# Thirty rows of wo a partition instead of thirty-one, and GpSimd loads part of the remainder

## The chip, the core and the metric

The kernel runs on one core of a Trainium2 chip. The core has five engines that are ordered among themselves only by semaphores: TensorE (PE, with weight loads shown as PEld), VectorE (DVE), ScalarE (ACT), GpSimd (POOL) and SyncE (SP, which only issues loads and stores here), and sixteen DMA engines that move data between the memory (HBM) and the core's own memory of 128 partitions. The metric is device time in microseconds: the median of several runs without a profiler. The profile is of one execution more.

## What is computed

One step of attention for 32 sequences (`B`), 32 query heads that share 8 key and value heads, head width 128, over the last 512 of 2048 cached positions, with a projection before (`wq`) and behind (`wo`):

```python
W = min(4096, max(256, Sk // 4))                      # 512
q = (x @ wq).reshape(B, Sq, Hq, Dh)                   # heads ahead of positions
k = jnp.repeat(k_cache[:, :, Sk - W:, :], rep, axis=1)
v = jnp.repeat(v_cache[:, :, Sk - W:, :], rep, axis=1)
p = softmax(einsum("bhqd,bhkd->bhqk", q, k) * Dh ** -0.5)
o = einsum("bhqk,bhkd->bhqd", p, v)
return o.reshape(B, Sq, Hq * Dh) @ wo                 # wo: 4096 rows of 512
```

All data are bf16. Nearly all bytes are the two caches (32 MB each); `wq` and `wo` have 4 MB each.

## The kernel before

The 32 sequences are worked in eight groups `q` of four (`NQ`). For each group there is a load `K{q}` of 4 MB into one of two buffers `K_sb`, and a load `V{q}` into one of two buffers `V_sb`; V5 to V7 are cut in two pieces. SyncE issues all of them in the order of the list `LOADS`, on one queue: a load is issued when its buffer is free (K waits for the transposes `T` of the group two before, V for the products `P` of the group two before), and the DMA engines work on loads in the order in which they were issued. SyncE's own order is therefore the order of all big loads: a wait in it holds back every load behind it.

VectorE transposes K (`KT_sb`, line 538), TensorE makes the scores (`S`, line 362), VectorE and ScalarE the softmax, TensorE turns the weights into value rows (`E`, line 376) and multiplies with V (`P`, line 388); VectorE and ScalarE copy the sums (`C_sb`), and a fold (`F`, lines 398 and 404) on TensorE and a copy `D` on ScalarE (line 598) bring the attention's output of the group into `o_sel`, laid out for the last projection. The order on each engine is written out in the lists at the top.

**The last projection.** Row `128 h + r` of `wo` belongs to head `h` and place `r` of its output. Partition `4 h + d` of `wo_sb` holds `NI` = 31 rows of head `h`, rows `31 d` to `31 d + 30`: 128 partitions, 124 rows of each head. `wo_sb` lies in the first K buffer, which is free once T6 is done; it is loaded in three pieces W0, W1, W2 of 21, 8 and 2 rows a partition (`WOP`), the last loads of the kernel. The `NX` = 4 rows of each head that are left over go to a tile `wx_sb` of their own, all four of a head in one partition, 4 KB. They are brought by seven small loads A0 to A6 (`EXTRA`: first head, last head, first partition), each of five heads (the last of two), to partitions that lie four apart. These stand in `LOADS` behind V5.1. `wx_sb` has rows in 32 partitions only; the rest is zero, by a memset on GpSimd early in the program (line 305), and the small loads wait for it (`pool_w`).

`fold` follows the same split: four matrices times 31 columns (`F_sb`, line 398) for the rows in `wo_sb`, and one matrix `F_x` (line 404) that puts each head's four remaining columns where `wx_sb` has its rows. GpSimd builds `F_x` with three copies (line 315). `o_sel` has `NI + NX` columns for each sequence.

At the end TensorE waits for the last copy D and for all small loads (`sem_wx`), multiplies with the `NX` rows of `wx_sb` (four products a row, line 485), then waits for W0, W1 and W2 in turn and multiplies with their rows. For W2 the products are ordered so that half of the output is finished first; VectorE and ScalarE copy a half each, and SyncE and ScalarE store them.

**GpSimd** builds masks and constants, and for each pair of groups copies the queries from `QT_sb` into `QBD` (line 328, sixteen copies; the last four wait for the scores of group 5). After those it has nothing to do. `QT_sb` holds 4096 elements a partition and is read by nothing else.

```python
EXTRA = [(5 * j, min(5 * j + 5, 32), j + 28 * (j // 4)) for j in range(7)]
WOP = [(0, 21), (21, 29), (29, 31)]
```

Of the kernel before, what the change touches and what calls it, by code (L numbers as in the profile page):

```python
# [5 lines left out]
BF16 = mybir.dt.bfloat16  # L6
# [22 lines left out]
ROUNDS = 3  # L29

LOADS = """
K0 K1 V0.0 K2 V1.0 K3 V2.0 K4 V3.0 K5 K6 V4.0 K7 V5.0 V5.1 A0 A1 A2 A3 A4 A5 A6 V6.0 V6.1 V7.0 V7.1 W0 W1 W2
""".split()

X_PARTS = [(0, 25), (25, 30), (30, 32)]
V_PIECES = 5 * [[0, 32]] + 2 * [[0, 16, 32]] + [[0, 18, 32]]
EXTRA = [(5 * j, min(5 * j + 5, 32), j + 28 * (j // 4)) for j in range(7)]
WOP = [(0, 21), (21, 29), (29, 31)]


def ops_of(text):
# [3 lines left out]
def bass_standalone__sliding_block_cached__sampling_kernel(  # L45
# [7 lines left out]
):  # L53
    B, Sq, D = x.shape
    _, HKV, SK, DH = k_cache.shape
    HD = wq.shape[1]
    HQ = HD // DH
# [3 lines left out]
    P = 128  # L61
# [2 lines left out]
    NQ = B // 4  # L64
    KB = 4
    R = W // KB
    NI = 31
    NX = DH - 4 * NI
    LAST = NQ - 1
    PIECES = 4  # L70
# [56 lines left out]
    with ExitStack() as es:  # L127
        sb = lambda name, shape, dt: es.enter_context(nc.sbuf_tensor(name, shape, dt))
        sem = lambda name: es.enter_context(nc.semaphore(name))
# [8 lines left out]
        QT_sb = sb("QT_sb", [P, 32, 2, HQ, 2], BF16)  # L138
# [3 lines left out]
        PTc = sb("PTc", [P, R, REP], BF16)  # L142
        C_sb = sb("C_sb", [P, 2, 4, DH], F32)
        o_sel = sb("o_sel", [P, NI + NX, 8 + B], BF16)
        wx_sb = sb("wx_sb", [P, NX, D], BF16)
        E_sb = sb("E_sb", [P, REP, 33, KB], BF16)
        F_pad = sb("F_pad", [P, 4 * (4 * HQ + 1)], F32)
        F_x = sb("F_x", [P, P], F32)
# [7 lines left out]
        wq_sb = V_sb[1][:, :].rearrange("p (kt n) -> p kt n", kt=DKT)  # L156
        wo_sb = K_sb[0][:, 0:NI * D].rearrange("p (i n) -> p i n", i=NI)

# [7 lines left out]
        F_hd = spare[:, 1792:1856].bitcast(F32)  # L166
# [9 lines left out]
        def folds(q):  # L176
            return (F_ps if q < LAST - 1 else O_ps[:, q - LAST + 1])[:, 0:4 * (NI + NX)].rearrange(
                "p (b i) -> p b i", b=4)
# [6 lines left out]
        sem_k = [sem(f"sem_k{i}") for i in range(2)]  # L185
        sem_v = [[sem(f"sem_v{i}_{j}") for j in range(max(len(v) for v in V_PIECES) - 1)] for i in range(2)]
        sem_wx = sem("sem_wx")
        sem_wo = [sem(f"sem_wo{i}") for i in range(len(WOP))]
        sem_out = sem("sem_out")
        names = (  # L190
# [3 lines left out]
        s = {n: sem(n) for n in names}  # L194
# [44 lines left out]
        @block.sync  # L239
        def _(sp):  # L240
            wait = Waits(sp)
            wo_h = wo.rearrange("(h r) n -> h (r n)", r=DH)
            wo_r = wo_h[:, 0:4 * NI * D].rearrange("h (d m) -> h d m", d=4)
            wx = wx_sb.rearrange("p a n -> p (a n)")
            for op in ops_of(" ".join(LOADS)):
                kind, q = op[0], op[1]
                if kind == "K":
                    if q == 2:
                        for key, n in BIAS.items():
                            sp.sem_inc(op_sem[key], n)  # L250
                    if q >= 2:
                        wait([ends["T", q - 2, 1]])
                    sp.dma_start(K_sb[q % 2][:, :], rows(k_cache, q)).then_inc(sem_k[q % 2], 16)
                elif kind == "V":
                    if q == 1:
                        sp.wait_ge(s["pe_q"], 8)
                    r0, r1 = (4 * g for g in V_PIECES[q][op[2]:op[2] + 2])
                    if q >= 2:
                        wait([ends["P", q - 2, r1 // 4 - 1]])
                    sp.dma_start(  # L260
                        V_sb[q % 2][:, r0 * DH:r1 * DH], rows(v_cache, q, r0, r1)
                    ).then_inc(sem_v[q % 2][op[2]], 16)
                    if q and len(V_PIECES[q]) == 2:
                        sp.sem_inc(sem_v[q % 2][1], 16)
                elif kind == "A":
                    h0, h1, p0 = EXTRA[q]
                    sp.wait_ge(s["pool_w"], 1)
                    sp.dma_start(
                        wx[p0:p0 + 4 * (h1 - h0) - 3:4, :], wo_h[h0:h1, 4 * NI * D:]
                    ).then_inc(sem_wx, 16)  # L270
                else:
                    wait([ends["T", NQ - 2, 1]])
                    i0, i1 = WOP[q]
                    sp.dma_start(
                        wo_sb[:, i0:i1, :].rearrange("p i n -> p (i n)"),
                        wo_r[:, :, i0 * D:i1 * D],
                    ).then_inc(sem_wo[q], 16)
            store(sp, 0)

        @block.gpsimd  # L280
        def _(pool):
            wait = Waits(pool)

            def diag(t, pattern, name):
                pool.memset(t, 0.0).then_inc(s[name], 1)
                pool.wait_ge(s[name], 1)
                pool.affine_select(
                    out=t, in_=t, compare_op=ALU.not_equal, fill=1.0,
                    base=0, pattern=pattern, channel_multiplier=1,
                ).then_inc(s[name], 1)  # L290

            diag(xsel[:, :, :], [[-1, 4], [-4, 32]], "pool_x")
            pool.memset(junk[:, :], 0.0).then_inc(s["pool_j"], 1)
            pool.memset(QBD[:, :, :, :], 0.0).then_inc(s["pool_q"], 1)
            diag(F_id[:, :, :], [[-1, HQ], [-32, 4]], "pool_f")
            diag(m_id[:, :, :, :], [[-4, HKV], [-32, 4], [-1, KB]], "pool_m")
            pool.memset(F_pad[:, :], 0.0).then_inc(s["pool_fz"], 1)

            diag(E_id[:, :, :].rearrange("p e (b h) -> p e b h", b=4),
                 [[-1, REP], [-4, 4], [-16, HKV]], "pool_ei")  # L300
            pool.memset(E_sb[:, :, :, :], 0.0).then_inc(s["pool_e"], 1)
            pool.wait_ge(s["pool_e"], 1)
            pool.wait_ge(s["pool_ei"], 2)
            pool.tensor_copy(E_sb[:, :, 0:32, KB - 1], E_id[:, :, :]).then_inc(s["pool_e"], 1)
            pool.memset(wx_sb[:, :, :], 0.0).then_inc(s["pool_w"], 1)
            pool.memset(F_x[:, :], 0.0).then_inc(s["pool_fz"], 1)
            pool.wait_ge(s["pool_e"], 2)
            pool.wait_ge(s["pool_fz"], 2)
            pool.wait_ge(s["dve_c"], 1)
            pool.tensor_copy(  # L310
                F_diag, F_hd.unsqueeze(1).to_broadcast([P, 4, HQ])
            ).then_inc(s["pool_fz"], 1)
            for h0, h1, p0 in ((0, 20, 0), (20, 30, 32), (30, 32, 34)):
                k = min(5, h1 - h0)
                pool.tensor_copy(
                    F_x[:, p0:p0 + 20].rearrange("p (k l) -> p l k", l=4)[:, 0:(h1 - h0) // k, 0:k],
                    F_hd[:, h0:h1].rearrange("p (l k) -> p l k", k=k),
                ).then_inc(s["pool_fz"], 1)
            pool.wait_ge(s["pool_q"], 1)
            pool.wait_ge(s["dve_QT"], 1)  # L320
            for q in range(0, NQ, 2):
                if q:
                    wait([ends["S", q - 1, 1]])
                for b in range(4):
                    pr = slice(32 * b, 32 * b + 32)
                    if q or b:
                        pool.wait_ge(s["pool_qbd"], 2 * q + b)
                    pool.tensor_copy(  # L328
                        QBD[pr].rearrange("p u a (h c) -> p u a h c", h=HKV).rearrange(
                            "p u (w t) h c -> p (u w) t h c", w=2)[:, :, :, :, 4 * b:4 * b + 4],  # L330
                        QT_sb[pr, q:q + 2].rearrange("p u w (h e) t -> p (u w) t h e", h=HKV),
                    ).then_inc(s["pool_qbd"], 1)

        @block.tensor
        def _(pe):
# [124 lines left out]
            with pe.Fori(0, ROUNDS) as j:  # L460
                for op, site in zip(rounds[0], steps):
                    waits = []
                    for key in sorted({key for w, _ in site for key in w}):
# [9 lines left out]
                        a, b = fits[-1]  # L473
# [4 lines left out]
            wait = Waits(pe)  # L478
            wait([ends["D", NQ - 1]])
            pe.wait_ge(sem_wx, 16 * len(EXTRA))  # L480

            def summed(i, rows, cs):
                for c in cs:
                    n = 2 * (c % 2) + c // 2
                    ins = pe.matmul(  # L485
                        Y_ps[32 * c:32 * (c + 1), 0:P],
                        lhsT=o_sel[:, i, 8:], rhs=rows[:, n * P:(n + 1) * P],
                        start=i == NI, stop=i == NI - 1, tile_position=(0, 32 * c),
                    )
                return ins  # L490

            for i in range(NX):
                summed(NI + i, wx_sb[:, i], range(4))
            for j, (i0, i1) in enumerate(WOP):
                pe.wait_ge(sem_wo[j], 16)
                last = j == len(WOP) - 1
                for cs in ((0, 1), (2, 3)) if last else (range(4),):
# [169 lines left out]
```

## Time and profile before

| | |
|---|---|
| time, median of 3 runs | 183.33 us (183.27 to 183.37) |
| time of the profiled execution | 183.41 us |
| its span, first to last instruction | 182.1 us |
| TensorE busy | 123.3 us (68%) |
| VectorE busy | 108.9 us (60%) |
| ScalarE, GpSimd busy | 46.8 us, 14.7 us |
| moved | 75.68 MB, 416 GB/s over the span |
| chain that ended last, by engine | DMA 52%, DVE 19%, PE 18%, issue 7% |

Times are from the first instruction on, the span lies inside the measured time, and the profiled execution was 0.08 us longer than the median. Where the profile shows the span in forty slices, each digit is the busy share of one slice (4.55 us) in tenths. A line of the chain of waits has start, duration and what was being worked on or waited for, in us. A line of the timeline has start, duration, engine, line of the kernel, operation, tile written and tiles read, count, and in brackets the idle time before it and what ended that.

### The profile page before, as it was taken

The numbers are of one execution on the slowest core, as the hardware profiler recorded it, in microseconds if no ns is written. First come the engines' busy times: TensorE is split into PE (matmuls) and PEld (weight loads), VectorE is DVE, ScalarE is ACT, GpSimd is POOL, SyncE is SP. The second block draws the span as 40 slices with busy tenths as digits, with TensorE's granted clock in tenths as the row PEclk, the third lists the DMA queues.
The fourth block names the chain that finished last, engine by engine and source line by source line (L and its number), as shares of the span: only waits on it lengthen the run. The fifth ranks groups of instructions, "written<-read, shape, count | busy, mean of one in ns | idle before, by whom it ended". The sixth has DMA issues, their size and how long they took to land.

```text
span 182.1 us, 3916 instructions
## 1 busy us (share of the span) xinstructions
PE 123.3 (68%) x1664; PEld 60.5 (33%) x1664; DVE 108.9 (60%) x103; ACT 46.8 (26%) x85; POOL 14.7 (8%) x39
## 2 busy tenths in 40 slices
PE   0029900444499879728992799645199899699984
PEld 0013300113135255205440355204035454354463
DVE  0022289849959950997079814997942499824030
ACT  3000310016014422601062014402006416327030
POOL 7910003000030000003000000002000000000000
PEclk9999995555559969965799559965559999999999
DMA  6998999999999999999999999999999999999992
GB/s 236 462 425 389 453 461 432 389 446 461 435 389 439 457 425 400 439 461 414 403 446 450 417 410 446 453 418 410 446 446 389 428 428 436 422 435 429 446 377 77
DMA packets 3523, 75.68 MB, mean 416 GB/s; under 512 B 444, under 2 KB 540, under 8 KB 700
## 3 DMA queue, kind: packets, MB, share of 16 engines
q1 hardware_dynamic: 3424, 75.52, 97.0%
q8 instruction: 7, 0.11, 0.3%
q10 hardware_dynamic: 92, 0.05, 0.1%
HBM read 75.53 MB, written 0.03 MB: 415 GB/s over the span
## 4 chain that ended last, share of the span: by engine, by line
DMA 52%; DVE 19%; PE 18%; issue 7%; ACT 1%; DVEq 1%; SPq 0%; ACTq 0%
DMA K_sb<-in_k_cache_dram 16%; DMA V_sb<-in_v_cache_dram 16%; DVE KT_sb L538 16%; DMA K_sb<-in_wo_dram 13%; PE ps L388 8%; DMA V_sb<-in_wq_dram 7%; PE ps L350 5%; PE ps L362 3%; DVE QT_sb L526 2%; PE ps L376 1%; PE ps L398 1%; ACT KT_sb L588 1%; PE ps L485 1%; DVEq L571 0%; DVE maxv L552 0%
## 5 line engine op out<-in xcount | busy, mean ns | idle before, releaser
L538 DVE STREAM_TRANSPOSE KT_sb<-K_sb 128x4096 f32<-128x4096 f32 x16 | 70.2, 4424 | 17.0 <-DMA K_sb<-in_k_cache_dram 16.9
L388 PE MATMUL ps<-V_sb,bd 32*128 32x512 bf16 x1024 | 66.5, 415 | 6.6 <-DMA V_sb<-in_v_cache_dram 6.6
L362 PE MATMUL ps<-KT_sb,QBD 128*32 128x512 bf16 x256 | 22.5, 487 | 29.4 <-DVE KT_sb L538 29.4
L388 PEld LDWEIGHTS ps<-V_sb,bd 32*128 32x128 bf16 x1024 | 27.0, 101 | 40.8 <-issue 10.5
L619 ACT ACTIVATE bd<-PTc,mask 128x512 bf16 x32 | 20.5, 710 | 1.5 <-ACT PTc L614 1.5
L362 PEld LDWEIGHTS ps<-KT_sb,QBD 128*32 128x32 bf16 x256 | 6.2, 108 | 43.2 <-DVE KT_sb L538 34.5
L605 ACT ACTIVATE P_f<-ps,negmax 128x512 f32<-128x512 f32 x8 | 5.5, 687 | 51.7 <-DVE negmax L554 51.7
L398 PE MATMUL ps<-C_sb,F_pad 128*128 128x124 f32 x64 | 12.6, 358 | 4.9 <-DVE C_sb L550 4.6
L614 ACT ACTIVATE PTc<-ps 128x512 bf16<-128x512 f32 x8 | 4.8, 597 | 39.7 <-PE ps L376 39.7
L328 POOL COPY QBD<-QT_sb 32x256 bf16<-32x256 bf16 x16 | 6.2, 390 | 105.1 <-PE ps L362 90.1
L398 PEld LDWEIGHTS ps<-C_sb,F_pad 128*128 128x128 f32 x64 | 10.7, 253 | 9.5 <-DVE C_sb L550 8.7
L571 DVE TENSOR_SCALAR bd<-PTc,mask 128x512 bf16 x32 | 8.9, 342 | 7.6 <-ACT PTc L614 7.6
L376 PE MATMUL ps<-P_bf,E_sb 128*128 128x128 bf16 x128 | 9.5, 234 | 2.6 <-DVE P_bf L561 2.6
L350 PE MATMUL ps<-V_sb,bd 128*128 128x512 bf16 x32 | 9.1, 456 | 2.0 <-DMA V_sb<-in_wq_dram 2.0
L376 PEld LDWEIGHTS ps<-P_bf,E_sb 128*128 128x128 bf16 x128 | 8.1, 105 | 6.9 <-DVE P_bf L561 3.5
L626 ACT ACTIVATE C_sb<-ps 32x512 f32<-32x512 f32 x14 | 8.2, 588 | 8.2 <-PE ps L388 8.1
L550 DVE COPY C_sb<-ps 32x512 f32<-32x512 f32 x12 | 8.3, 693 | 2.9 <-PE ps L388 2.6
L339 PE MATMUL ps<-bd 32*128 32x128 bf16 x4 | 0.6, 294 | 10.6 <-DMA bd<-in_x_dram 10.6
L552 DVE TENSOR_REDUCE maxv<-ps 128x1 f32<-128x512 f32 x8 | 5.5, 691 | 3.6 <-PE ps L362 3.4
L578 DVE COPY C_sb<-ps 32x512 f32<-32x512 f32 x4 | 2.8, 693 | 8.1 <-PE ps L388 8.0
L510 DVE CAST bd<-ps 128x512 bf16<-128x512 f32 x1 | 0.7, 691 | 11.2 <-PE ps L339 11.2
L521 DVE CAST KT_sb<-ps 128x1024 bf16<-128x1024 f32 x2 | 2.4, 1224 | 7.1 <-PE ps L350 7.1
(37 smaller groups left out, 44.1 us busy)
## 6 DMA issues: line engine op xcount, KB each, us to landing
K_sb<-in_k_cache_dram SPq DMA_DIRECT2D x8, 4096.0 KB, 22.5
V_sb<-in_v_cache_dram SPq DMA_DIRECT2D x5, 4096.0 KB, 26.4
V_sb<-in_v_cache_dram SPq DMA_DIRECT2D x4, 2048.0 KB, 21.5
V_sb<-in_wq_dram SPq DMA_DIRECT2D x1, 4096.0 KB, 12.3
K_sb<-in_wo_dram SPq DMA_DIRECT2D x1, 2688.0 KB, 21.7
V_sb<-in_v_cache_dram SPq DMA_DIRECT2D x1, 2304.0 KB, 14.2
V_sb<-in_v_cache_dram SPq DMA_DIRECT2D x1, 1792.0 KB, 15.8
K_sb<-in_wo_dram SPq DMA_DIRECT2D x1, 1024.0 KB, 23.5
```

The costliest lines, as they stand in the source:

```text
L328: pool.tensor_copy(QBD[pr].rearrange("p u a (h c) -> p u a h c", h=HKV).rearrange("p u (w t) h c -> p (u w) t h c", w=2)[:, :, :, :, 4 * b ...
L350: ins = pe.matmul(ps[:, n], lhsT=xT_sb[:, kt, :], rhs=wq_sb[:, kt, n * 512:(n + 1) * 512], start=kt == 0, stop=kt == DKT - 1, tile_positio ...
L362: ins = pe.matmul(S_ps[32 * c:32 * c + 32, :], lhsT=QBD[:, q % 2, 2 * w + t, c0:c0 + 32], rhs=KT_sb[:, w, :, KB * h:KB * h + KB, t], start ...
L376: ins = pe.matmul(EP_ps[:, e * R:(e + 1) * R], lhsT=window[:, KB - 1 - k:KB - 1 - k + P], rhs=P_bf[:, k * R:(k + 1) * R], start=k == 0, st ...
L388: ins = pe.matmul(sums_of(b, q), lhsT=bd[pr, q % 2, 4 * g:4 * g + 4].rearrange("p r h e -> p (r h e)"), rhs=V_sb[q % 2][pr, 512 * g:512 * ...
L398: ins = pe.matmul(folds(q)[:, :, 0:NI], lhsT=F_sb[:, d].rearrange("p h d -> p (h d)"), rhs=C_sb[:, q // LAST, :, NI * d:NI * d + NI], star ...
L538: dve.transpose(KT_sb[:, w].bitcast(F32).rearrange("p r c t -> p r (c t)"), K_sb[i].bitcast(F32).rearrange("p (r w c) -> p r w c", r=R, w= ...
L550: dve.tensor_copy(*pick_args(r)).then_inc(op_sem["ANY", "C"], 1)
L552: dve.tensor_reduce(maxv[:, :], S_ps, AX.X, ALU.max).then_inc(s["dve_m"], 1)
L571: ins = dve.tensor_scalar(bd[:, bass.ds(odd, 1), :, h, :].rearrange("p o r e -> p (o r) e"), PTc[:, :, :], mask[:, h:h + 1], None, op0=ALU ...
L619: ins = act.activation(bd[:, bass.ds(odd, 1), :, h, :].rearrange("p o r e -> p (o r) e"), PTc[:, :, :], ACTF.Copy, scale=mask[:, h:h + 1])
L626: act.activation(*pick_args(r), ACTF.Copy).then_inc(op_sem["ANY", "C"], 1)
```

## The change

`NI` becomes 30, so `wo_sb` has 120 rows of each head, W0 has 20 rows a partition instead of 21, and `NX` is 8. A head's eight remaining rows are 8 KB in one partition.

`wx_sb` is no tile of its own any more but the memory of `QT_sb`. Its memset, twice as wide, moves from GpSimd's start to behind the last copy into `QBD`, for which it waits (`pool_qbd` 16).

The small loads on SyncE become five, A0 to A4: five heads each for heads 0 to 19, and four for heads 24 to 27. The rows of the other eight heads, 20 to 23 and 28 to 31, are brought by one load that GpSimd issues, to partitions 60 to 67. Its source has the form 2 x 4 x 8 KB. Ahead of it and behind it GpSimd issues a load of seven rows of 64 bytes into a scratch tile `passed`, which nothing reads; GpSimd waits for both at its end. TensorE waits for GpSimd's load too (`sem_w2`) before it multiplies with `wx_sb`. `F_x` follows the new partitions with three copies as before.

```diff
-K0 K1 V0.0 K2 V1.0 K3 V2.0 K4 V3.0 K5 K6 V4.0 K7 V5.0 V5.1 A0 A1 A2 A3 A4 A5 A6 V6.0 V6.1 V7.0 V7.1 W0 W1 W2
+K0 K1 V0.0 K2 V1.0 K3 V2.0 K4 V3.0 K5 K6 V4.0 K7 V5.0 V5.1 A0 A1 A2 A3 A4 V6.0 V6.1 V7.0 V7.1 W0 W1 W2
...
-EXTRA = [(5 * j, min(5 * j + 5, 32), j + 28 * (j // 4)) for j in range(7)]
-WOP = [(0, 21), (21, 29), (29, 31)]
+EXTRA = [(5 * j, 5 * j + 5, j) for j in range(4)] + [(24, 28, 32)]
+PASSED = (7, 7)
+WOP = [(0, 20), (20, 28), (28, 30)]
...
-    NI = 31
+    NI = 30
...
-        wx_sb = sb("wx_sb", [P, NX, D], BF16)
+        wx_sb = QT_sb[:, :, :, :, :].rearrange("p j w h t -> p (j w h t)").rearrange("p (a n) -> p a n", n=D)
+        passed = sb("passed", [16, 32], BF16)
...
-            pool.memset(wx_sb[:, :, :], 0.0).then_inc(s["pool_w"], 1)
...
-            for h0, h1, p0 in ((0, 20, 0), (20, 30, 32), (30, 32, 34)):
-                k = min(5, h1 - h0)
-                pool.tensor_copy(
-                    F_x[:, p0:p0 + 20].rearrange("p (k l) -> p l k", l=4)[:, 0:(h1 - h0) // k, 0:k],
-                    F_hd[:, h0:h1].rearrange("p (l k) -> p l k", k=k),
-                ).then_inc(s["pool_fz"], 1)
+            for to, of in (
+                (F_x[:, 0:20].rearrange("p (k l) -> p l k", l=4),
+                 F_hd[:, 0:20].rearrange("p (l k) -> p l k", k=5)),
+                (F_x[:, 32:48].rearrange("p (k l) -> p k l", l=4)[:, :, 0], F_hd[:, 24:28]),
+                (F_x[:, 60:68].rearrange("p (a g) -> p a g", a=2),
+                 F_hd[:, 16:32].rearrange("p (a g) -> p a g", a=2)[:, :, 4:8]),
+            ):
+                pool.tensor_copy(to, of).then_inc(s["pool_fz"], 1)
...
+            pool.wait_ge(s["pool_qbd"], 16)
+            pool.memset(wx_sb[:, :, :], 0.0).then_inc(s["pool_w"], 1)
+            for n, (a, k) in enumerate(zip((0, 8), PASSED)):
+                pool.dma_start(
+                    passed[a:a + k, :], wo[a:a + k, 0:32]
+                ).then_inc(sem_pass[n], 16)
+                if n == 0:
+                    pool.wait_ge(s["pool_w"], 1)
+                    pool.dma_start(
+                        wx_sb.rearrange("p a n -> p (a n)")[60:68, :],
+                        wo.rearrange("(a g r) n -> a g (r n)", a=4, g=8)[2:4, 4:8, 4 * NI * D:],
+                    ).then_inc(sem_w2, 16)
+            for each in sem_pass:
+                pool.wait_ge(each, 16)
...
             pe.wait_ge(sem_wx, 16 * len(EXTRA))
+            pe.wait_ge(sem_w2, 16)
```

More of the change, by code (lines that the diff above doesn't have):

```diff
@@ L187, in bass_standalone__sliding_block_cached__sampling_kernel @@
         sem_wx = sem("sem_wx")
+        sem_pass = [sem(f"sem_pass{i}") for i in range(len(PASSED))]
+        sem_w2 = sem("sem_w2")
         sem_wo = [sem(f"sem_wo{i}") for i in range(len(WOP))]
```

## The prediction

> **What bounds the kernel now.** I read the page's rows of the sixteen DMA engines first, then the chain of waits in order of time, then the last microseconds of TensorE and the queue of SyncE.
>
> ```profile
> DMA  6998999999999999999999999999999999999992
> q1 hardware_dynamic: 3424, 75.52, 97.0%
> q8 instruction: 7, 0.11, 0.3%
> ```
>
> The DMA engines are busy to nine tenths or more from the third slice to the last but one, and the queue of SyncE and its loads (q1) is 97.0% of sixteen engines' span. So the kernel ends when its last load has landed and a short tail has run. The chain of waits shows the tail:
>
> ```profile
> 155.27 0.32 SPq L274
> 155.59 0.04 issue
> 155.63 23.50 DMA K_sb<-in_wo_dram
> 179.13 0.04 issue
> 179.17 0.97 PE ps L485 x40
> 180.14 0.02 issue
> 180.16 0.27 ACT P_bf L634
> ```
>
> W1, the second of the three loads of wo, lands at 179.13 us. TensorE does 32 products with it and 8 with W2, and the output is copied and stored. The same end on TensorE (start, duration, operation, idle time before):
>
> ```profile
> 177.30 0.41 PE L485 MATMUL ps<-wx_sb,o_sel 128*32 128x128 bf16 x16 [0.38 <-ACT o_sel L598]
> 177.53 1.35 PE L485 MATMUL ps<-K_sb,o_sel 128*32 128x128 bf16 x84
> 179.17 0.90 PE L485 MATMUL ps<-K_sb,o_sel 128*32 128x128 bf16 x40 [0.29 <-DMA K_sb<-in_wo_dram]
> ```
>
> The single records inside these rows: four products start every 56 ns. The last of W0's 84 starts at 178.66, so TensorE could go on at 178.70 and stands still until 179.17. W1's 32 products start from 179.17 to 179.58. The last 8 start at 179.77, because W2 lands at 179.73. W2's last part sets the end.
>
> A load lands in sixteen parts, one for each DMA engine, and the trace keeps the arrival of each. K0's sixteen parts arrive within 0.47 us (22.25 to 22.72). W2's lie 2.06 us apart, in three groups: five **free** parts (177.67 to 178.15), five **row** parts (178.72, 178.75, 178.81, 178.95, 179.23) and six **fetch** parts (179.37, 179.39, 179.40, 179.42, 179.55, 179.73). Two things made the groups. Each of the instruction packets (16 KB, q8) holds up the engine that carries it: it takes 1.06 us, and the 32 KB packet after it takes 1.71 instead of 1.21. After the one at 48.8 us fifteen parts of K2 arrive from 51.39 to 51.86 and one at 53.21; by V5.1, after five such packets, eleven parts arrive from 148.59 to 149.05 and five from 150.29 to 150.68. A sixth comes at 174.2. The other thing is the seven loads of a few rows, queued just behind V5.1: in V6.0, the load after them, five of the eleven early parts are 0.95 to 1.11 us later than their fellows, which is six or seven packets of 4 KB at the 159 ns that each takes. So a load of five rows uses five engines, the same five each time, and none of them is one that fetched.
>
> **The change, part by part.**
>
> *W0 is a row shorter in every partition.* Each engine serves eight partitions, so each loses 8 KB. Packets of 21,504 and 8,192 bytes take 801 and 309 ns: 0.037 ns a byte, 38 ns for 1 KB, 0.30 us for eight packets. W1 and W2 keep their sizes, so every part of both arrives 0.30 earlier. The latest, a fetch part, has nothing added: 179.73 becomes 179.43.
>
> *The row loads.* Five loads of 8 KB rows replace seven of 4 KB rows. The two engines that carried seven packets (1.11 us) carry five of 309 ns (1.55): +0.43, less 0.30, is +0.13. Two that carried six (0.95) get +0.59 less 0.30, +0.29; the last carries four (1.24), +0.28 less 0.30, -0.02. The latest row part (179.23; its slip of 1.11 in V6.0 marks it as one of the seven-packet engines) becomes 179.36. The others end at 179.10 or earlier. So the row parts catch up with the fetch parts but don't pass them.
>
> *GpSimd's load.* Eight rows of 8 KB in two shares put four packets, 4 x 309 = 1.24 us, on two engines. On free ones their parts arrive at 178.15 - 0.30 + 1.24 = 179.09 at the latest: hidden behind 179.43. On engines that are late already they set the end (first rival). The trace has no load issued by GpSimd, so which engines take the shares is its largest unknown. What it shows: six fetches fell on six different engines, none a row engine. That looks like a rotation, which would leave the free five side by side, and neighbours share a fate; and rows ahead that move the start on may move it past the row engines. I take free engines, a little over even.
>
> By the Trainium skill's "DMA: Bandwidth & Descriptors", section "Why a DMA increments its semaphore by 16 and not by 1", a load from SyncE takes the lowest-numbered engines, as many as divide both sides' slowest dimension, and one from GpSimd takes consecutive engines from a cursor that moves round. The five slipped parts of V6.0 agree with the first half; no run here shows the second. By it the seven tiny rows lead the shares to the eighth and ninth engines, if the cursor began at the first, and the sum is what it is above if those two are free.
>
> *The two loads of seven tiny rows.* They put one packet of 64 bytes and some completion writes on an engine. Below: nearly nothing (a 4-byte write takes 9 ns, a 512-byte packet 28). Above: what an instruction packet costs beyond its bytes. It made its engine's part 1.53 late where 16 KB of a load take 0.61, so 0.92. The 1 KB packets of x, sent from another queue between wq's packets, left gaps of 34 to 90 ns. In kind and size these are nearest; I take 0.03, and keep 0.92 as a rival.
>
> *GpSimd and SyncE.* The memset of wx (1.91 us at 6.95) leaves the start, where GpSimd then waits for VectorE until 12.25 anyway: nothing. It returns twice as wide behind the last copies of QBD:
>
> ```profile
> 122.55 1.74 POOL L328 COPY QBD<-QT_sb 32x256 bf16<-32x256 bf16 x4 [37.33 <-PE ps L362]
> ```
>
> and here is what SyncE does at that time:
>
> ```profile
> 122.42 5.10 SPq L268 DMA_DIRECT2D wx_sb<-in_wo_dram  x7
> 138.72 16.22 SPq L260 DMA_DIRECT2D V_sb<-in_v_cache_dram  x4
> ```
>
> The memset runs from 124.3 to about 128.0 (twice 1.8 to 1.9). The row loads, which wait for it, are issued from 128.0 to 131.6 (five at 5.10/7 = 0.73). Queued behind them is V6.0, which waits for TensorE until 138.72: 7 us of cover. Were that gone, V6.0's first packets would still have until about 148.6, when the engines are through with V5.1. GpSimd's own three issues, at 0.5 to 0.9 us each by SyncE's rows or several times that, end forty microseconds before 177.3, when TensorE wants the rows; nothing on its queue waits behind them but the end. VectorE transposes while GpSimd writes: its sixteen transposes took 4.40 to 4.45 us each, GpSimd's copies beside one or not, so nothing.
>
> *TensorE.* 16 products more with wx and 4 fewer with W0: three groups of 56 ns, 0.17. The folds have four columns fewer in eight instructions and 16 more in two: nothing. The copy of o_sel has 152 columns for 140: 0.03 at most. TensorE is ready for W1 at 178.70 + 0.20 = 178.90 instead of waiting; W1's latest part comes at 179.13 - 0.30 = 178.83. Its products end by 179.35, before W2's 179.43. The cover here is 0.1 us: with a gain much above 0.3, TensorE would set the end.
>
> **The sum.** -0.30 + 0.03 = -0.27 on the profiled execution: 183.41 becomes 183.14, its span 182.1 becomes 181.8. The median shown is 183.33, 0.08 under that execution, so the forecast is 183.06 (-0.15%). Its own range, with 0.1 to 0.2 for a lag of the engines that differs between runs, is 182.85 to 183.25. A difference under 0.2%, 0.37 us, is about what a measurement of this kernel can't tell from none.
>
> **The rivals.**
>
> *The shares fall on late engines.* On a fetch engine a share makes W2's part 179.37 to 179.73, less 0.30, plus 1.24: 180.31 to 180.67. On a row engine it is 180.60 for the latest and about 180.3 for the others. It decides from any engine whose part is now later than 179.73 + 0.30 - 1.24 = 178.79, or that gets longer rows besides: eleven of the sixteen. The end comes 0.55 to 0.95 later; V7.1's latest part moves from 170.25 to 171.5 at most, and TensorE, 1.24 later, still reaches W1 at 180.1, before W2. With the later of two shares counting, I take +0.8: 184.1. For it: only five of sixteen engines are free, and nothing in the trace names them. Against: the rotation.
>
> *GpSimd's loads cost every engine what a fetch costs beyond its bytes.* 179.43 + 0.92 = 180.35, +0.62: 183.95. For it: the instruction packets. Against: the packets of x, and that all three are over forty microseconds before the end, though a lag stays once it is there, as K2's late part shows.
>
> *The change doesn't do what it says: the eight rows go one to an engine, from the first.* The latest row part becomes 179.36 + 0.31 = 179.67, with the tiny packets 179.70 against 179.73: 183.30. The same page and section tells of such a spread: some loads from GpSimd take all sixteen engines, with an even number of partitions on each. No run here shows it.
>
> **How the numbers follow.** Forecast 0.52, of which 0.20 ends more than 0.37 us under 183.33 (lags that shrink more than the sum has them) and 0.32 within; late engines 0.30; a cost on every engine 0.12; spread rows 0.06. So faster 0.20, same 0.38, slower 0.42. The time is the forecast's; the range reaches from its lower bound to the first rival's upper one, 182.85 to 184.3.
>
> **What would show it.** Right: W2's parts in two groups instead of three, the latest near 179.45, and two parts near 179.0 that were early; TensorE's wait before W1 gone or under 0.1; V6.0 issued near 138.7 as before. The first rival: one or two parts of every load after about 130 us 1.2 later than the others of their group, and past 180 at the end. The second: all sixteen later together. The third: eight parts with 0.3 more, none with 1.24. I am wrong in the bound itself if W2 lands 0.3 earlier and the end doesn't move, or if SyncE issues V6.0 late.

## The result: 1% slower, and the profile after

| | before | after |
|---|---|---|
| median | 183.35 us (183.27 to 183.51, 4 runs) | 185.25 us (185.08 to 185.36, 4 runs) |
| ratio to before | | 1.0102 (95% interval 1.0084 to 1.0119) |
| profiled execution, its span | 183.41, 182.1 us | 185.08, 183.6 us |
| W2's latest part | 179.73 us | 181.19 us |

The page of the changed kernel has nearly the same row of DMA engines, a little less in q1, and one queue more:

```profile
DMA  6999999989999999999999999999999999999981
GB/s 234 458 450 400 407 457 457 443 378 436 453 450 428 382 450 453 428 407 418 457 439 414 407 450 450 428 421 414 457 364 364 432 425 428 437 428 423 440 365 55
q1 hardware_dynamic: 3408, 75.45, 96.7%
q8 instruction: 7, 0.11, 0.2%
q0 software_dynamic: 144, 0.07, 0.1%
```

In the row of GB/s, two slices in a row show 364; each is 4.6 us, so they are the time from 133 to 142 us. Before the change no slice between the second and the tail was under 389. The DMA engines are as busy as ever in these slices and move less. The chain of waits ends as before, 1.4 to 1.5 us later:

```profile
157.82 22.73 DMA K_sb<-in_wo_dram
180.56 0.04 issue
180.60 0.63 PE ps L505 x32
181.23 0.00 issue
181.24 0.37 PE ps L505 x8
```

TensorE's end (start, duration, idle time ahead in brackets): the wait for W1 did not go, it grew from 0.29 to 0.40 us.

```profile
178.46 0.63 PE L505 MATMUL ps<-QT_sb,o_sel 128*32 128x128 bf16 x32 [0.39 <-ACT o_sel L618]
178.91 1.29 PE L505 MATMUL ps<-K_sb,o_sel 128*32 128x128 bf16 x80
180.60 0.94 PE L505 MATMUL ps<-K_sb,o_sel 128*32 128x128 bf16 x40 [0.40 <-DMA K_sb<-in_wo_dram]
```

Around the moved memset, on GpSimd, SyncE and VectorE:

```profile
124.23 3.51 POOL L339 MEMSET QT_sb<- 128x4096 bf16 x1
...
128.35 0.59 POOL L346 DMA_DIRECT2D QT_sb<-in_wo_dram  x1
...
127.77 3.67 SPq L272 DMA_DIRECT2D QT_sb<-in_wo_dram  x5
138.48 18.65 SPq L264 DMA_DIRECT2D V_sb<-in_v_cache_dram  x4
...
124.90 3.13 DVE L581 TENSOR_SCALAR P_bf<-P_f,recip 128x512 bf16<-128x512 f32 x1
```

SyncE issues V6.0 when it did before. VectorE's product with `recip` takes 3.13 us beside the memset; the seven others of its kind take 0.49.

**Where the 1.46 us on W2 come from.** The arrivals of the parts split it. (The trace doesn't name the engine of a packet. On a busy engine a packet starts within some 10 ns of the end of the one before, and by that the records of one engine can be joined.) Fourteen of W2's parts come by 180.32, two at 181.18 and 181.19. Two things are added up here.

First, every engine lost time while GpSimd's rows were under way. The eight packets of 8 KB run in four rounds, one on each of two engines, at 134.8, 136.5, 138.2 and 140.0 us. In the same time K7's 32 KB packets, on all sixteen engines, take some 1.46 us instead of 1.21, until 141 us; beside the first round it is 1.39. The stretch comes some tenths of a microsecond behind the record of a round: the packet from 135.66 to 136.88 has the second round's record (136.47 to 136.79) inside it and still takes 1.22, and the next on its engine takes 1.47. So each round holds up all engines for 0.17 to 0.25 us. Two engines that carry no share lose 0.1 us more (packets of 1.54 to 1.57); that they are the ones that fill partitions 60 to 67 would fit, but is not shown. K7's earliest parts come at 139.49 instead of 138.81, V5.1's at 149.53 instead of 148.59, and the fourteen parts of W2 at 180.32 where 179.43 was forecast: +0.89.

Second, the two engines that carry the shares are not free ones. Their records hold the four packets of GpSimd and, at 150 us, the five packets of SyncE's row loads. The two loads of seven tiny rows both ran on the same seven engines, and these two are among them. The share and the longer rows together make their parts 0.87 later than the rest. -0.30 + 0.89 + 0.87 = +1.46.

### The profile page after: what moved, and what is told of

It is laid out like the page before. It is cut to its first block, busy times and chain, and to the rows that moved or that the text cites. A ratio compares the mean times of both kernels' runs of the same rounds, so it can differ in the third digit from the quotient of the medians.

```text
span 183.6 us, 3943 instructions
## 1 busy us (share of the span) xinstructions
PE 124.1 (68%) x1676; PEld 61.2 (33%) x1676; DVE 111.5 (61%) x103; ACT 46.8 (26%) x85; POOL 18.1 (10%) x42
## 4 chain that ended last, share of the span: by engine, by line
DMA 62%; DVE 14%; PE 12%; issue 8%; DVEq 1%; SPq 1%; ACT 1%; ACTq 0%
DMA K_sb<-in_k_cache_dram 29%; DMA V_sb<-in_v_cache_dram 14%; DMA K_sb<-in_wo_dram 12%; DVE KT_sb L558 11%; DMA V_sb<-in_wq_dram 7%; PE ps L369 5%; PE ps L407 5%; DVE QT_sb L546 2%; PE ps L381 1%; ACT KT_sb L608 1%; PE ps L395 1%; PE ps L505 1%; DVE maxv L572 0%; SPq L278 0%; SPq L257 0%
## 5 line engine op out<-in xcount | busy, mean ns | idle before, releaser
L407 PE MATMUL ps<-V_sb,bd 32*128 32x512 bf16 x1024 | 67.7, 419 | 7.7 <-DMA V_sb<-in_v_cache_dram 7.5
L381 PE MATMUL ps<-KT_sb,QBD 128*32 128x512 bf16 x256 | 22.0, 479 | 29.9 <-DVE KT_sb L558 29.9
L407 PEld LDWEIGHTS ps<-V_sb,bd 32*128 32x128 bf16 x1024 | 27.5, 102 | 42.7 <-issue 12.2
L417 PE MATMUL ps<-C_sb,F_pad 128*128 128x120 f32 x64 | 12.8, 362 | 3.8 <-DVE C_sb L570 3.5
L581 DVE TENSOR_SCALAR P_bf<-P_f,recip 128x512 bf16<-128x512 f32 x8 | 6.5, 816 | 0.9
```

The lines of the kernel that those rows point to most:

```text
L381: ins = pe.matmul(S_ps[32 * c:32 * c + 32, :], lhsT=QBD[:, q % 2, 2 * w + t, c0:c0 + 32], rhs=KT_sb[:, w, :, KB * h:KB * h + KB, t], start ...
L407: ins = pe.matmul(sums_of(b, q), lhsT=bd[pr, q % 2, 4 * g:4 * g + 4].rearrange("p r h e -> p (r h e)"), rhs=V_sb[q % 2][pr, 512 * g:512 * ...
L417: ins = pe.matmul(folds(q)[:, :, 0:NI], lhsT=F_sb[:, d].rearrange("p h d -> p (h d)"), rhs=C_sb[:, q // LAST, :, NI * d:NI * d + NI], star ...
L581: dve.tensor_scalar(P_bf[:, :], P_f32[:, :], recip[:, :], None, op0=ALU.mult).then_inc(done("N"), 1)
```

## The experiments

Ratios are to the kernel before on the same chip, with their 95% intervals.

### The rows without GpSimd, and GpSimd's tiny loads without the rows

`e1_sp_rows`:

```diff
-K7 V5.0 V5.1 A0 A1 A2 A3 A4 V6.0
+K7 V5.0 V5.1 A0 A1 A2 A3 A4 A5 A6 V6.0
...
+[(20, 24, 32), (24, 28, 33), (28, 32, 34)]      # EXTRA behind the first four
-            for n, (a, k) in enumerate(zip((0, 8), PASSED)):
...
-            pe.wait_ge(sem_w2, 16)
```

> The changed kernel without any load from GpSimd: the eight heads' rows come by two more small loads from SyncE (four heads each, seven small loads in all, partitions 32 to 47). The changed kernel's trace shows all sixteen parts of K7 0.7 to 1.0 us later than before, while GpSimd's rows are under way. Theory 'GpSimd's load stalls every engine': without it K7's parts are back at 138.8 to 139.05 and 140.5 to 140.9, W0 is 0.30 us shorter for every part, and the end is set by the four engines that carry seven rows of 8 KB (7 x 0.309 = 2.16 us instead of 1.11): 179.23 + 1.05 - 0.30 = 179.98 us for W2, time 183.6. Rival 'the memset, or the late transposes behind it, do it' (VectorE's product with recip took 3.13 us beside the memset instead of 0.49): K7's parts stay late, time 184.5.

183.76 us, ratio 1.0018 (1.0008 to 1.0028). K7's parts are back at 138.93 to 139.25 and 140.51 to 140.81, with the memset and its 3.12 us product still there. W2's latest four parts come at 179.90 to 180.02, where 179.98 was worked out. So the memset isn't the cause, and the prices of the shorter W0 and of an 8 KB row hold.

`e2_tiny_only`, the kernel before with:

```diff
+            for n, a in enumerate((0, 8)):
+                pool.dma_start(
+                    passed[a:a + 7, :], wo[a:a + 7, 0:32]
+                ).then_inc(sem_pass[n], 16)
```

> The kernel before with GpSimd's two loads of seven tiny rows alone, issued at the same place as in the changed kernel; nothing else differs. Theory 'GpSimd's queue as such costs every engine': K7's parts come 0.4 to 0.9 us later, 183.8 to 184.3. Rival 'only the eight rows of 8 KB do': K7's parts as before, 183.4 to 183.5; the upper figure if the 0.15 us by which the changed kernel's time outside its span grew (1.32 to 1.47) belongs to the use of that queue.

183.42 us, 1.0005 (0.9996 to 1.0015), K7's parts as before. GpSimd's queue by itself costs nothing that can be measured; the rows of 8 KB do.

### Where the rows are written

`e3_own_ports`:

```diff
-EXTRA = ... + [(24, 28, 32)]
+EXTRA = ... + [(24, 28, 40)]
...
-                        wx_sb.rearrange("p a n -> p (a n)")[60:68, :],
+                        wx_sb.rearrange("p a n -> p (a n)")[32:40, :],
```

> The changed kernel with GpSimd's eight rows sent to partitions 32 to 39 instead of 60 to 67, and the last small load of SyncE to partitions 40, 44, 48 and 52 instead of 32, 36, 40 and 44. In the changed kernel the two engines that carry GpSimd's rows are two of the five that carry SyncE's rows, and they write into partitions that two other engines fill during K7. By the Trainium skill's 'DMA: Bandwidth & Descriptors', section 'The descriptor swizzle', the first two engines write partitions 0 to 7 and 32 to 39 of a load of 128 partitions, and 60 to 67 belong to the eighth and ninth. Theory 'crossing': a row that goes to partitions which another engine fills stalls all of them, so here K7's parts are as early as before the change, and the end is set by the two engines with five rows and a share, 179.36 + 1.24 = 180.6 us for W2; SyncE's last load now crosses, for up to 0.25; 184.3 to 184.6. Rival 'any packet of 8 KB from GpSimd's queue stalls all': no difference to the changed kernel, 185.25.

184.55 us, 1.0064 (1.0047 to 1.0081): inside the range of the first theory. K7's parts come at 138.82 to 139.18 and up to 140.75; its packets take 1.21 to 1.23 while the shares run. W2's last two parts come at 180.67 and 180.70, where 180.6 was worked out for the two engines with both kinds of rows. SyncE's last small load, which now crosses, stretches a packet of every engine by 0.15 to 0.3 at 151 us.

The same stretch from 134 to 141 us, while GpSimd's rows are under way, in the views by stretches. First the changed kernel, then this one, then the first experiment, which has no such load (columns: stretch, length, busy time and count of PE, PEld, DVE, ACT, POOL, granted clock, busy share of the DMA engines, GB/s):

```profile
134.00:141.00 7.00, 7.00 (x108) 3.37 (x104) 3.84 (x5) 3.15 (x5) 0.00 (x0) 0.82 0.95 344
```

```profile
134.00:141.00 7.00, 7.00 (x132) 3.46 (x124) 4.18 (x6) 3.57 (x6) 0.00 (x0) 1.00 0.95 405
```

```profile
134.00:141.00 7.00, 7.00 (x104) 3.35 (x100) 3.89 (x5) 3.15 (x5) 0.00 (x0) 0.80 0.95 407
```

The DMA share is 0.95 in all three: a packet that is held up counts as busy time. Of the two DMA columns only the last tells them apart, 344 against 405 and 407 (414 before the change).

`e4_cross_sp`, the kernel before with the rows of head h in partition h:

```diff
-EXTRA = [(5 * j, min(5 * j + 5, 32), j + 28 * (j // 4)) for j in range(7)]
+EXTRA = [(5 * j, min(5 * j + 5, 32), 5 * j) for j in range(7)]
...
-                        wx[p0:p0 + 4 * (h1 - h0) - 3:4, :], wo_h[h0:h1, 4 * NI * D:]
+                        wx[p0:p0 + h1 - h0, :], wo_h[h0:h1, 4 * NI * D:]
```

> The kernel before with head h's four remaining rows in partition h instead of partitions that lie four apart: the same seven loads from SyncE, the same bytes on the same engines, but each load's rows now go to neighbouring partitions, which one or two engines fill in a big load. Theory 'crossing': stalls of all engines during the seven loads, half as long as the changed kernel's 0.25 us (rows of 4 KB, not 8), 0.1 to 0.9 us in all, 183.45 to 184.25. Rival 'the software queue is what stalls, not the place written': 183.35, no change.

183.96 us, 1.0032 (1.002 to 1.0045). No load comes from GpSimd, the engines carry the same bytes, and still all of them are slowed: packets of V6.0 that take 0.61 take up to 1.08, and V6.0's parts come 0.75 later than before. The stretch of the seven loads, before the change and here:

```profile
148.00:153.00 5.00, 4.84 (x88) 2.47 (x84) 5.00 (x2) 3.15 (x5) 0.00 (x0) 1.00 1.03 436
```

```profile
148.00:153.00 5.00, 4.04 (x72) 2.00 (x68) 5.00 (x2) 3.16 (x5) 0.00 (x0) 1.00 1.01 354
```

`e8_share_sync`, the changed kernel's load of eight rows, the same in form and place, from SyncE:

```diff
+                elif kind == "B":
+                    sp.dma_start(
+                        wx[60:68, :],
+                        wo.rearrange("(a g r) n -> a g (r n)", a=4, g=8)[2:4, 4:8, 4 * NI * D:],
+                    ).then_inc(sem_w2, 16)
```

> The changed kernel with the very same load of eight rows (same source form, same partitions 60 to 67) issued by SyncE behind its last small load; GpSimd issues none. Theory 'crossing and late engines, whatever queue the load comes from': it is cut into the same two shares on the first two engines, the four rounds of it stall every engine for about 0.25 each, now between V5.1 and V6.0, and the two engines end last: 185.0 to 185.4, K7's parts as before the change. Rival 'GpSimd's queue is part of it': no stalls, 180.6 us for W2, 184.2 to 184.4.

185.5 us, 1.012 (1.0104 to 1.0137). The stall has moved with the load, and K7 is untouched:

```profile
134.00:141.00 7.00, 7.00 (x108) 3.32 (x104) 3.89 (x5) 3.15 (x5) 0.00 (x0) 0.82 0.98 419
...
148.00:153.00 5.00, 4.78 (x88) 2.40 (x84) 5.00 (x2) 3.16 (x5) 0.00 (x0) 1.00 1.02 338
```

Fourteen parts of W2 come by 180.54 and two at 181.34 and 181.82. Both halves of the loss stay when GpSimd's queue is out of it. (The four rounds of about 0.25 each that were expected were too tidy: here packets of all engines are stretched by 0.1 to 0.66 in a row, about 1 us in all.)

### Can the shares be steered to other engines

`e5_steer_7`, `e6_no_tiny` and `e7_steer_8` change only the tiny loads around GpSimd's rows, and e7 their place (64 to 71, with `F_x` to match). In short:

```diff
-PASSED = (7, 7)
+PASSED = (2, 2, 2, 1) ahead, (2, 2, 2, 1) behind     # e5
+PASSED = () ahead, () behind                         # e6
+PASSED = (2, 2, 2, 2) ahead, (2, 2, 2) behind        # e7
```

> The changed kernel with another set of tiny loads on GpSimd: ahead of the eight rows three loads of two rows and one of one row instead of one load of seven, and the same four behind them. In the changed kernel both loads of seven rows, and the two shares, lie on the same first seven engines. Theory 'a load that is cut in two moves the start by two, a load of seven doesn't move it': the shares now go to the eighth and ninth engines, which write partitions 60 to 67 themselves and carry none of SyncE's rows: K7's parts as early as before the change, W2's latest part at 179.45 to 179.55, time 183.05 to 183.2. Rival 'the start never moves': the shares stay on the first two engines, K7's parts 0.7 to 1.0 late, 185.2 to 185.4.

> The changed kernel without both loads of seven tiny rows; GpSimd issues only the load of the eight rows. Theory 'the seven rows don't steer the shares': the same engines, the same stalls, 185.1 to 185.3. Rival 'they move the start by seven': the shares now lie elsewhere than in the changed kernel, and the latest two parts of W2 change by 0.5 us or more.

> The changed kernel with four loads of two tiny rows ahead of the eight rows, three behind, and the eight rows sent to partitions 64 to 71. If loads that are cut in two move the start by two, the shares go to the ninth and tenth engines, which write these partitions themselves. No stalls then; the time says whether the tenth engine is one that an instruction packet has made late: free, 183.05 to 183.2; late, 179.4 to 179.7 + 1.24 - 0.30 = 180.3 to 180.7 us for W2, 183.9 to 184.3. Rival 'the start never moves': the first two engines again, writing where two others write, 185.2 to 185.4.

185.47 (1.0119, 1.0102 to 1.0136), 185.53 (1.0127, 1.0107 to 1.0147) and 185.3 us (1.0102, 1.0085 to 1.0118): nothing was steered. In e7's records the loads of two rows all lie on one and the same pair of engines, and so do the shares of 8 KB; that pair also carries SyncE's rows. In e6, without tiny loads, the two engines with shares again carry SyncE's rows, and W2's two latest parts come at 181.47, the rest by 180.45: 1.02 apart, 0.86 in the changed kernel. My theory that a load cut in two moves the start by two fell. In partitions 64 to 71 the eight rows hold up the engines too: while they run, 16 KB packets take up to 0.95 us where they otherwise take 0.61.

### The memset, and a queue held up

`e9_memset_later`, the first experiment with one wait ahead of the memset, and `e11_memset_n5`, the same with the group before:

```diff
+            wait([ends["N", NQ - 2]])      # e9: product of group 6
+            wait([ends["N", NQ - 3]])      # e11: product of group 5
```

> The first experiment's kernel (no load from GpSimd, seven small loads of 8 KB rows from SyncE) with the memset of wx put behind VectorE's product with recip of group 6, so that the two no longer run side by side. Theory 'the product's 2.6 us beside the memset are hidden': it takes 0.49 us again and the time stays that of the first experiment, 183.6 to 183.85. Rival 'they cost time': 183.35 to 183.5.

191.34 us, 1.0421 (1.0394 to 1.0448). I had named the wrong group. The product of group 6 is at 146 us, so the memset, the small loads that wait for it and all loads behind them on SyncE came late:

```profile
150.13 4.93 SPq L272 DMA_DIRECT2D QT_sb<-in_wo_dram  x7
155.11 2.53 SPq L264 DMA_DIRECT2D V_sb<-in_v_cache_dram  x4
```

```profile
GB/s 226 442 440 440 440 440 440 440 427 406 423 427 416 434 430 440 440 437 427 440 430 434 413 427 420 427 440 434 440 406 423 95 102 382 434 436 413 455 382 45
```

V6.0 is issued at 155.1 instead of 138.7, and the DMA engines run dry: two slices of 4.8 us at 95 and 102 GB/s. It says nothing of the memset, but shows what the row loads' wait costs once its cover is gone: some 7.6 us more than the first experiment. It shows one thing more: once the engines have run dry, the sixteen parts of V6.0 come within 0.61 us (162.29 to 162.90), so the lag that instruction packets leave on an engine is gone.

> The first experiment's kernel with the memset of wx behind VectorE's product of group 5, the one that ran beside the memset at 124.9 us (the run before this put it behind the product of group 6, at 146 us, too late for the small loads). The memset now runs from about 125.4 to 128.9, beside the transposes of K7. Theory 'hidden': the product takes 0.49 us, the transposes stay at 4.4, SyncE issues its small loads until about 134 and V6.0 at 138.5 as before; time as the first experiment's, 183.6 to 183.85. Rival 'the stretched product cost time': 183.35 to 183.5.

184.08 us, 1.0038 (1.0025 to 1.0052). The product is back at 0.49 us, the two transposes beside the memset take their 8.77 together, V6.0 goes out at 138.8, and W2's latest part comes at 180.09 (180.02 in the first experiment).

```profile
125.30 0.49 DVE L569 TENSOR_SCALAR P_bf<-P_f,recip 128x512 bf16<-128x512 f32 x1
125.73 8.77 DVE L546 STREAM_TRANSPOSE KT_sb<-K_sb 128x4096 f32<-128x4096 f32 x2
...
125.90 3.51 POOL L340 MEMSET QT_sb<- 128x4096 bf16 x1 [1.33 <-DVE P_bf L569]
```

So the stretched product was hidden: taking it away gained nothing. Why the time is 0.3 above the first experiment's is open; the two ran on different chips, W2 explains 0.07 of it, and the span 0.1.

### What the shorter W0 is worth, and rows on their own partitions

`e10_no_rows`, which leaves the last eight rows of wo of every head out of the product:

```diff
-K7 V5.0 V5.1 A0 A1 A2 A3 A4 V6.0
+K7 V5.0 V5.1 V6.0
...
-            pe.wait_ge(sem_wx, 16 * len(EXTRA))
-            pe.wait_ge(sem_w2, 16)
+            pe.wait_ge(s["pool_w"], 1)
```

> The changed kernel without any of the small loads, neither SyncE's nor GpSimd's: the last eight rows of wo of every head are left out of the product. What is left is the shorter W0 alone. Theory 'the engines that carried an instruction packet set the end before, and a row less in W0 is worth 0.30 us to them': W2's latest part at 179.4 to 179.5, time 183.0 to 183.1, 0.1 to 0.2% faster. Rival 'the five row engines set the end before': W2 at 178.8 or earlier, 182.4.

183.06 us, 0.9986 (0.9977 to 0.9995). W2's parts fall into two groups, the latest at 179.33. TensorE hardly waits any more:

```profile
177.29 0.63 PE L492 MATMUL ps<-QT_sb,o_sel 128*32 128x128 bf16 x32 [0.39 <-ACT o_sel L605]
177.75 1.93 PE L492 MATMUL ps<-K_sb,o_sel 128*32 128x128 bf16 x120
```

The view joins all 120 products of W0, W1 and W2 in one row. In the single records only the last eight, which start at 179.37, come some 0.05 us late. This is as far as the shorter W0 can go: with no rows to bring at all it gains 0.14%, and TensorE, with 0.05 us to spare, is then the next bound.

`e12_eight_heads`, thirty rows a partition, all from SyncE, each row on partitions that, by the map of the third experiment, its own engine fills:

```diff
+EXTRA = [(5 * j, 5 * j + 5, j) for j in range(4)] + [(20, 28, 32), (28, 32, 33)]
```

> Thirty rows a partition without GpSimd: SyncE loads five heads at a time for heads 0 to 19 as in the changed kernel, heads 20 to 27 in one load of eight rows four partitions apart, and heads 28 to 31 in one of four. Every row goes to partitions that its engine also fills in the big loads. Theory 'no crossing, no stall; W2 ends with the engines that carry most': four engines carry six rows of 8 KB (1.85 us), one five, three one; the latest row part is 179.23 + 1.85 - 1.11 - 0.30 = 179.67, against 179.43 for the parts of engines that fetched: 183.2 to 183.3, between nothing and 0.1% better than before. Rival 'the load of eight lands on an engine that fetches late': 179.42 + 0.31 - 0.30 = 179.43, which changes nothing; a stall would show as 183.5 or more.

183.45 us, 1.0009 (1.0000 to 1.0018). No stall, W2's latest part at 179.73, the old value and 0.06 above the sum: the engines with six rows have given back what W0 gained. It doesn't beat the kernel before, and no run that computes everything did.

## Why the prediction was wrong, step by step

**The bound** was right: the end follows W2's latest part in all of these kernels; in the one without rows TensorE is only 0.05 us ahead of it.

**W0 a row shorter, -0.30**: right. Without the rows W2's latest part came at 179.33 (forecast 179.43) and the time at 183.06.

**The row loads**: the price of 0.31 us for a packet of 8 KB held to 0.04 (180.02 against 179.98 in the first experiment). In the changed kernel the engines that ended last carried a share of GpSimd's load besides.

**"I take free engines, a little over even"** is the first step that failed. The shares went to two of the five engines that carry SyncE's rows; that was the first rival's mechanism. Its price, 0.55 to 0.95 us, was counted from the old end, 179.73. Of the changed kernel's +1.46 the stall is 0.89, which leaves +0.57 for it; in the third experiment, where K7 isn't stalled, the two parts come at 180.67 and 180.70, +0.97, with a stretch of SyncE's last small load in it. The argument from the rotation of the instruction packets was about other transfers than the ones in question. What the trace did show of loads with few rows, that SyncE's use the same engines each time, holds for GpSimd's too. The rule of the Trainium skill's "DMA: Bandwidth & Descriptors", section "Why a DMA increments its semaphore by 16 and not by 1", that GpSimd's loads start from a cursor that moves round, is not what these runs show: with none, with seven, or with pairs of rows ahead, the two shares lay where SyncE's rows lie. The measurement decides.

**The two loads of tiny rows, 0.03**: right in size (the second experiment: 0.06, no change within its interval). The upper bound I had set beside it, 0.92 on every engine, came close to the measured +0.89 by luck: the reason is one that the prediction did not have. The second rival laid it to GpSimd's queue; the tiny loads alone did nothing, and the same stall came from SyncE. **What the prediction left out is where the rows are written.** It counted what each engine carries and never asked which engine's partitions the rows go to; it put this at nothing, and it cost +0.89. In the kernel before, each row load's rows lie four partitions apart, and the fourth experiment shows what that is worth: put side by side, the same rows hold up all engines. Eight rows in partitions 60 to 67 hold up everyone; in 32 to 39, again carried by two engines of SyncE's rows, they don't. The Trainium skill's "DMA: Bandwidth & Descriptors", section "The descriptor swizzle", gives the map of engines to partitions on which the third experiment was laid out, and its section "Back-pressure in remote DMA" says for transfers between cores that a saturated port of the core's memory holds up other engines on the same path. That fits; the runs show the stall and its dependence on place. That another engine fills the place is taken from the map, since no trace here names an engine.

**The cases** were set up as rivals of each other, 0.30 and 0.12, with prices of +0.8 and +0.62 taken alone. Both losses came together, and the range's upper bound, 184.3, was the first rival's alone, so the time lies above it. The two losses hang together: that the shares lie on engines of SyncE's rows makes them late, and those engines, as far as it can be told, don't fill partitions 60 to 67.

**VectorE, "nothing"**: wrong in the number, 2.6 us on one product, and harmless; the row I leaned on (transposes beside copies) was of another operation. **SyncE's queue**: right, V6.0 went out at 138.5, and the row loads were done by 131.4 (forecast 131.6). **TensorE**: right that it has little to give, as the run without rows shows.

The time grew by 1.9 us and the span of the profiled execution by 1.5. Between the two profiled executions the time grew by 1.67; the changed kernel's was the shortest of its four, which is most of the rest. What lies outside the span was 1.3 us before and 1.5 after; runs without any load from GpSimd had 1.3 to 1.6. That part is not explained.

## What to carry to other kernels

When a small transfer goes beside a stream that fills all DMA engines, ask two questions of it: which engine carries it, and whose partitions it writes. Read both from the arrivals of the parts and from GB/s by stretch, since the busy share stays at 0.95 or more while all engines are held up. When two rivals hang on the same unknown, add them up for the end of the range.

## What the runs showed of the hardware that was not expected

- Where a few rows are written decided whether they held up all sixteen DMA engines. Eight rows of 8 KB in partitions 60 to 67, beside a stream that fills all engines, cost every engine about 0.9 us (344 GB/s instead of 405 over 7 us), and about 1 us when they came from SyncE; in 32 to 39 nothing. 32 rows of 4 KB in neighbouring partitions cost 0.75 us; four partitions apart the stretch ran at 436 GB/s instead of 354. That such rows go to partitions which another engine is filling fits all of these and rests on the map.
- Loads of two or seven rows issued by GpSimd did not take turns over the engines: within an execution they lay on the same ones each time, and the two engines of a load cut in two were among SyncE's five.
- A memset on GpSimd stretched VectorE's product with one factor a partition (bf16 from f32, 128x512) from 0.49 to 3.13 us, but not the transposes: in `e11_memset_n5` two of them beside the memset took 8.77 us together, as without it.
- An instruction packet of 16 KB makes its DMA engine some 1.5 us late for as long as the stream keeps the engines busy: in K2, one part at 53.16 in the changed kernel beside fifteen from 51.39 to 51.93. In `e9_memset_later` the lag is gone once the engines have run dry.
